# Weight sums of the seven products spread over one batch, a sliced visit one slot later, and loads and transposes in another order

## The chip, the cores and the metric

The kernel runs on one core of a Trainium2 chip. The metric is the device time of one execution in microseconds (us). Five engines take part, each with its own instruction queue: TensorE (PE, with its weight loads shown as PEld), VectorE (DVE), ScalarE (ACT), GpSimd (POOL) and SyncE (SP), which here only issues transfers.

## The reference

Eight batches of eight heads, 512 tokens of width 64 and 32 state rows per head. Tokens and state read each other by softmax attention in both directions; the two results are concatenated (544 rows per batch) and go through a feed-forward layer of width 2048 whose activation is Mish, all in float32.

```python
scores = scale * np.matmul(x, state.transpose(0, 1, 3, 2))
a = softmax(scores);  xread = np.matmul(a, state)
scores2 = scale * np.matmul(state, x.transpose(0, 1, 3, 2))
a2 = softmax(scores2); sread = np.matmul(a2, x)
x = concat(xread, sread) -> (8 * 544, 512)
h = x @ w_in                          # 512 -> 2048
g = h * np.tanh(softplus(h))          # Mish
return g @ w_out                      # 2048 -> 512
```

## The kernel before

**Precision.** Every float32 matrix product is made of three products of rounded parts: high by high, high by low, low by high. A tile and its two parts appear as `g`, `gh`, `gl` (activations), `wo` and `wx` (w_out, parts and sums), `swh`, `swl` (state times w_in) and `ah`, `al` (attention weights).

**First product.** xread @ w_in is never formed from xread: `sw_slice` multiplies a batch's state by a slice of w_in (tile `swp`), and a slot's first product (tile `ph`, 12 matmuls per slot, steps G0 and G1) multiplies the attention weights by that. For batches from 2 on w_in comes back from a DRAM copy (`load_w_in_again`, tile `w_in`, 1 MB each), two loads at a time through the tag `raw` with two buffers. The same two buffers also hold the next batch's `x_in`, its transposed form `x_turned` and its moved form `x_rows`, in this order of use: x_in, x_turned, x_rows, then the w_in loads w4, w5, w2, w3. A load can only be issued when the user of its buffer two places earlier is done.

**Slots and the table.** The work of a batch is written out in `TABLE` as eight lines, the slots, one for each pair of 128-wide parts of the feed-forward width. Each step name starts or continues one generator. The same name again means its next stage: `S4 S4 S4` is matmuls, then the copy to `swh` on ACT, then the subtraction to `swl` on DVE. PE, DVE, ACT and POOL keep the order of the program (class `InOrder`); transfers on SP are placed by the scheduler at compile time, behind what they depend on. Steps that matter here:

- G0 G1: first product into `ph`; M0 M1: Mish from `ph` on ACT, which frees the `ph` bank (two banks in all).
- A, B: half of the second product. In batch 1 these are plain products into `acc`; from batch 2 on, units `(batch, p, j)` are consumed one per A or B, as fast as they are ready.
- P, p: prepare such a unit: `gh` on ACT, `gl` on DVE and, for a unit with seven products, sums of its blocks on POOL (tile `sums`).
- S4, S6: slices of `sw` for the running batch; N0, N2: for the next. A visit S4 uses load w4.
- X0 to X3, XD: transposes of the next batch's x on DVE, and eight small transfers that move it (`x_rows`, line 305); ST: its state blocks; SC: its scores; EE, EX: exponentials on ACT (they need another activation table than Mish); NO: normalisation; PR: `at`, `ah`, `al`.
- TU (and `tu` for the batch before): `e2_turned`, two transposes on DVE into `u` and sixteen small transfers into `e2T` (line 402), which sr0 and sr1, the state reads, need two or three slots later.
- lx, li, w2 to w5: loads of x, of x_in with the state rows, and of w_in.

**Seven products.** Where a unit's j is under `sevens(key, p)`, its second product is made of seven 256-wide products in place of four 512-wide ones with two blocks each. This needs sums of weight blocks, which `seven_weights(j)` (steps T; five calls j = 0 to 4 in all) makes once for the whole kernel in three stages: an addition on DVE and four operations on POOL (tile `w_sums`, one buffer); two copies on ACT (`wo`, `wx`); two subtractions on DVE. The products of a unit are collected in four PSUM banks, and `sums_of` combines the banks `one` and `two` (a copy on ACT and three operations on DVE) before the last unit's result is added.

```python
    def sevens(key, p):
        return FIRST if (key, p) == (2, 0) else SEVEN
```

The trace gives line 74 for all operations on PE, DVE, ACT and POOL (the helper in `InOrder`), so they are told apart by tile names.

Of the kernel before, what the change touches and what calls it, by code (L numbers as in the profile page):

```python
# [17 lines left out]
P = 128  # L18
B, H, S, NS, D = 8, 8, 512, 32, 64
# [5 lines left out]
SLOTS = NFC // 2  # L25
# [2 lines left out]
WARM = 5  # L28
UNITS = 10
SEVEN = 5  # L30
FIRST = 3
G = 4 * P


# [18 lines left out]
def quad(q):  # L53
    return slice(q * NS, (q + 1) * NS)
# [27 lines left out]
def state_attention_mish_kernel(ctx, tc, x, state, w_in, w_out, out):  # L82

    nc = tc.nc
# [20 lines left out]
    def second_bank(name):  # L105
        return ps_acc.tile([P, 512], F32, tag="acc", name=name)
# [167 lines left out]
    def attention(b, sn, x_in=None):  # L274
# [115 lines left out]
        def e2_turned():  # L390

            both = pool.tile([P, NC, 2, NT, NS], F32, tag="e2T", name=f"e2T_{b}", bufs=1)
            for kc in range(2):
                e2T[kc] = both[:, :, kc]
            u = pool.tile([P, 4, 2, NT * NS], F32, tag="sc" if b else "u0", name=f"u_{b}", bufs=1)
            for kc in range(2):
                dve.transpose(
                    u[:, :, kc].rearrange("i q (t n) -> i t q n", t=NT),
                    e2s[kc].rearrange("n (t q p) -> n t q p", t=NT, q=4))
            for c in range(NC):  # L400
                for q in range(4):
                    nc.sync.dma_start(  # L402
                        both[quad(q), c].rearrange("p k t n -> p (k t n)"), u[quad(c), q].rearrange("i k m -> i (k m)"))

        two = range(2)
# [90 lines left out]
        def sread(kc):  # L496
# [18 lines left out]
        own = dict(  # L515
            x=x_transposed, st=lambda _: state_blocks(b, sn() if b == 1 else sn) if b else state_blocks_0(sn), sc=lambda _: scores() if b else scores_q(), tr=soft1_t, ex=soft1_x,
            no=lambda _: soft1_n(), pr=soft1_a, mm=soft2_m, ee=soft2_e, sr=sread, xd=lambda _: x_moved(), tu=lambda _: e2_turned(), fill=fill, aT=aT)

        def soft2():
            for kc in two:  # L520
                soft2_m(kc)
                whole(soft2_e(kc))

        own.update(soft1=soft1, parts=soft1_parts, soft2=soft2, turn=e2_turned)
        return own

# [348 lines left out]
    S1, S3, S2, S4 = range(3, 7)  # L875
    T3, T4, T2 = range(3)
# [23 lines left out]
    def products(j, n7):  # L900

        left, right = slice(0, 256), slice(256, 512)
        if j < n7:
            return [
                (A11, "one", left, wo[j][:, 0, :, left]), (S2, "one", right, wx[0][:, j, :, T2]),
                (S3, "two", left, wx[0][:, j, :, T3]), (S1, "two", right, wo[j][:, 0, :, right]),
                (A12, "top", left, wo[j][:, 1, :, left]), (S4, "top", right, wo[j][:, 1, :, right]),
                (A22, "end", left, wx[0][:, j, :, T4])]  # L910
        return [
            (a, bank, slice(0, 512), wo[j][:, k])
            for bank, blocks in (("top", (A11, A12)), ("end", (A21, A22))) for k, a in enumerate(blocks)]
# [7 lines left out]
    def sevens(key, p):  # L921
        return FIRST if (key, p) == (2, 0) else SEVEN

# [38 lines left out]
    def sums_of(key, p, banks):  # L962

        e = banks["sums"] = pool.tile([P, 4, 256], F32, tag="wt", name=f"sums_{key}_{p}", bufs=1)
        one, two = (banks[n].rearrange("t (h e) -> t h e", h=2) for n in ("one", "two"))
        act.copy(e[:, 0], one[:, 0])
        dve.tensor_sub(e[:, 3], e[:, 0], one[:, 1])
        dve.tensor_add(e[:, 1:3], two, e[:, 3:].to_broadcast([P, 2, 256]))
        dve.tensor_add(e[:, 3], e[:, 1], two[:, 1])

    def consume():

        unit = ready.pop(0)
        key, p, j = unit
        hi, lo = parts.pop(unit)
        if j == 0:
            spans[key, p] = {n: second_bank(f"acc_{key}_{p}_{n}") for n in ("one", "two", "top", "end")}
        banks = spans[key, p]
        n7 = sevens(key, p)
        if j == max(n7, SLOTS - 1 if (key, p) != (B - 1, 1) else 0):  # L980
            sums_of(key, p, banks)
        for i, (a, bank, to, w) in enumerate(products(j, n7)):
            for n, (g, h) in enumerate(((hi, 1), (hi, 0), (lo, 1))):
                fresh = (key, p, bank) not in begun_banks
                begun_banks.add((key, p, bank))
                last["PE"] = pe.matmul(
                    banks[bank][:, to], g[:, a], w[:, h], start=fresh,
                    stop=(n == 2 and (j == SLOTS - 1 and i % 2 == 1 or j == n7 - 1 and i < 4)), skip_group_check=True)
            if j == n7 - 1 == SLOTS - 1 and (i, n) == (3, 2):
                sums_of(key, p, banks)  # L990
            if j == SLOTS - 1 and i == (5 if n7 > j else 1):
                result(key, 2 * p, banks["top"], banks["sums"][:, ::2], ALU.add)
            if j == SLOTS - 1 and i == (6 if n7 > j else 3):
                result(key, 2 * p + 1, banks["end"], banks["sums"][:, 1::2], ALU.subtract)
    def result(key, t, acc, sums, op):

        acc = acc.rearrange("t (h e) -> t h e", h=2)
        for h in ((slice(0, 1), slice(1, 2)) if (key, t) == (B - 1, NT - 1) else (slice(0, 2),)):
            dve.tensor_tensor(sums[:, h], acc[:, h], sums[:, h], op)
            store(key, t, sums[:, h], out.rearrange("r (h e) -> r h e", h=2)[:, h], nc.scalar if h.start else nc.sync)  # L1000

    def half_slot(key, j, at):


        if pending:
            second((2, 3) if at else (0, 1), not at)
        elif ready and (ready[0][:2] != (key, 0) or ready[0][2] < j + (j == SLOTS - 1 and at)):
            consume()

    TABLE = {  # L1010
        1: """
            G0 M0 G1 M1 mm0 mm1 ee0 ee1 A h l X0 X1 ee0 ee1 X2 X3 XD w0
            G0 M0 G1 M1 h S2 S2 S2 B l tu ST w1
            G0 M0 G1 M1 h A B l
            G0 M0 G1 M1 h A SC sr0 sr1 S4 S6 SC sr0 sr1 S4 S4 S6 S6 lx B l MM0 MM1
            G0 M0 G1 M1 h A TR0 TR1 w2 B l TR0 TR1 T0
            G0 M0 G1 M1 EE0 EE1 EX0 EX1 h A w3 B l NO EE0 EE1 T0 T0 NO
            G0 M0 G1 M1 h A PR0 PR1 TU B l T1
            G0 M0 G1 M1 h PR0 PR1 A N0 N2 PR0 PR1 N0 N0 N2 N2 B l T1 T1 li""",
        2: """  # L1020
            G0 M0 G1 M1 X0 X1 T2 A X2 X3 XD T2
            G0 M0 G1 M1 B ST w4 A T2
            G0 M0 G1 M1 SC sr0 sr1 S4 SC sr0 sr1 S4 S4 w5 lx B P MM0 MM1 p P p
            P G0 M0 p G1 M1 P p TR0 TR1 A P TR0 TR1 p B
            P G0 M0 p G1 M1 P p A EE0 EE1 EX0 EX1 P EE0 EE1 w2 p B NO
            P G0 M0 p G1 M1 P p S6 A P NO S6 S6 w3 p B
            P G0 M0 p G1 M1 P p PR0 PR1 TU T3 A P p B T3
            P G0 M0 p T3 G1 M1 P p PR0 PR1 P A P N0 N2 PR0 PR1 N0 N0 N2 N2 p li B""",
        3: """
            P G0 M0 p G1 M1 P p X0 X1 A P X2 X3 XD p B  # L1030
            P G0 M0 p T4 G1 M1 P p ST A P T4 p w4 B T4""",
        "steady": """
            P G0 M0 p G1 M1 P p X0 X1 A P X2 X3 XD p B
            P G0 M0 p G1 M1 P p ST A P p w4 B
# [9 lines left out]
            P G0 M0 p G1 M1 P p A P SC sr0 sr1 S4 SC sr0 sr1 S4 S4 p w5 lx B MM0 MM1  # L1044
            P G0 M0 p G1 M1 P p TR0 TR1 A P TR0 TR1 p B
            P G0 M0 p G1 M1 rm P p EE0 EE1 EX0 EX1 A EE0 EE1 P rm w2 p B NO
            P G0 M0 p G1 M1 P p NO A TU P S6 S6 S6 w3 p B
            P G0 M0 p G1 M1 P p PR0 PR1 A P p B
            P G0 M0 p G1 M1 P p PR0 PR1 A P SR0 SR1 N0 N2 SR0 SR1 rs PR0 PR1 N0 N0 N2 N2 rt p W0 W1 B""",
        B - 1: """  # L1050
# [16 lines left out]
    for key in [*range(1, B - 1), "s", B - 1]:  # L1067
        if key == "s":
            for i, item in enumerate(items):
                j, r, k = i // 4, i // 2 % 2, i % 2  # L1070
# [92 lines left out]
    while ready or todo:  # L1163
        begin()
        end()
        consume()
# [24 lines left out]
```

## Time and profile before

| | |
|---|---|
| median of 3 runs | 650.94 us (650.73 to 653.28) |
| the profiled execution | 652.01 us, of which the span of the trace is 650.2 us |
| PE busy | 631.5 us (97%), granted clock 0.995 on average |
| DVE busy | 429.7 us (66%) |
| ACT busy | 311.2 us (48%) |
| POOL busy | 136.0 us (21%) |
| chain that ended last | PE 81%, DVE 9%, DMA 4%, SP's queue 3%, ACT 2% |

PE is busy nearly all the time, but a busy PE can run at half its clock, and its matmuls are pipelined. So the useful reading is the start-to-start time of the same group of matmuls at different places, with the waits that PE has between them.

### The profile page before, as it was taken

Reading aid. Unit: us, or ns where it says so; the run is one execution under the profiler, and the core shown is the slowest. Engines: PE = TensorE matmul, PEld = TensorE weight load, DVE = VectorE, ACT = ScalarE, POOL = GpSimd, SP = SyncE. Lnnn points to the kernel's source line nnn. Section 1 sums busy time; section 2 is a strip of 40 time slices with the busy share of each in tenths; the row PEclk is TensorE's granted clock in tenths of the full one; section 3 lists DMA queues with packets and bytes.
Section 4 is the critical chain, followed back from the end, with each engine's and each line's share of the span. In section 5 each row is a group of like instructions: output and inputs, shape, how many; then the busy total and the mean of one; then the engine's idle time right before and its main releaser. Section 6 shows DMA issues by size and latency. Waiting matters only on the chain.

```text
span 650.2 us, 12856 instructions
## 1 busy us (share of the span) xinstructions
PE 631.5 (97%) x5090; PEld 526.6 (81%) x5090; DVE 429.7 (66%) x737; ACT 311.2 (48%) x638; POOL 136.0 (21%) x215
## 2 busy tenths in 40 slices
PE   8999999999989989999999999999999899999997
PEld 5776787687768678888888798888888798888996
DVE  6998975568447696768476666748485776634263
ACT  5998763254235443725255433735272575424240
POOL 0000000022410434313222141405031131413130
PEclk9999999999979999999999999999999999999999
DMA  8999914701681256324562257125631240101000
GB/s 323 410 358 306 322 35 132 218 1 37 161 298 28 65 148 202 121 71 125 140 225 66 69 160 236 34 85 153 189 135 47 73 140 23 34 1 28 6 33 32
DMA packets 70123, 85.64 MB, mean 132 GB/s; under 512 B 13744, under 2 KB 48560, under 8 KB 70064
## 3 DMA queue, kind: packets, MB, share of 16 engines
q1 hardware_dynamic: 69632, 84.63, 40.5%
q8 instruction: 40, 0.66, 0.4%
q10 hardware_dynamic: 432, 0.20, 0.1%
q14 instruction: 19, 0.16, 0.1%
HBM read 59.70 MB, written 13.11 MB: 112 GB/s over the span
## 4 chain that ended last, share of the span: by engine, by line
PE 81%; DVE 9%; DMA 4%; SPq 3%; ACT 2%; issue 1%; POOL 0%; DVEq 0%; ACTq 0%
PE ph L74 23%; PE acc_top L74 12%; PE acc L74 11%; PE acc_end L74 9%; PE acc_two L74 6%; PE acc_one L74 6%; PE swp L74 4%; PE ph_s L74 3%; SPq L402 3%; DVE gl L74 2%; DMA wir<-in_moe_w_in_dram 2%; DVE swl L74 2%; DVE sums L74 1%; PE acc_s_top L74 1%; PE srp L74 1%; PE sc L74 1%
## 5 line engine op out<-in xcount | busy, mean ns | idle before, releaser
L74 ACT ACTIVATE u<-ph 128x256 f32<-128x256 f32 x192 | 63.1, 383 | 119.1 <-PE ph L74 112.3
L74 POOL TENSOR_TENSOR sums<-u 128x256 f32<-128x256 f32 x58 | 45.8, 789 | 267.8 <-DVE gl L74 266.7
L74 PE MATMUL acc_top<-wo,gh 128*128 128x256 f32 (+1 forms) x384 | 92.5, 329 | 0.0
L74 PE MATMUL ph<-ah,swh 128*128 128x512 f32 (+1 forms) x260 | 80.4, 391 | 1.8 <-DVE swl L74 1.0
L74 PE MATMUL acc<-wo,gh 128*128 128x512 f32 x256 | 81.3, 399 | 0.0
L74 PE MATMUL ph<-al,swh 128*128 128x512 f32 (+1 forms) x260 | 79.6, 388 | 0.2 <-DVE al L74 0.2
L74 PE MATMUL ph<-ah,swl 128*128 128x512 f32 (+1 forms) x260 | 79.6, 388 | 0.0
L74 PEld LDWEIGHTS acc_top<-wo,gh 128*128 128x128 f32 x384 | 63.3, 191 | 8.3 <-issue 2.1
L74 DVE TENSOR_TENSOR gl<-u,gh 128x384 fp32r<-128x384 f32 (+1 forms) x96 | 60.3, 629 | 13.3 <-ACT gh L74 9.1
L74 POOL TENSOR_TENSOR sums<-sums,u 128x128 f32<-128x128 f32 x116 | 63.5, 547 | 9.1
L74 DVE CAST gh<-u 128x512 fp32r<-128x512 f32 x38 | 17.9, 470 | 71.5 <-ACT u L74 47.5
L74 PE MATMUL acc_top<-wo,gl 128*128 128x256 f32 (+1 forms) x192 | 62.6, 326 | 0.1
L74 PEld LDWEIGHTS acc<-wo,gh 128*128 128x128 f32 x256 | 48.1, 191 | 13.6 <-issue 3.3
L74 PEld LDWEIGHTS ph<-al,swh 128*128 128x128 f32 x260 | 48.5, 188 | 10.7 <-DVE al L74 0.4
L74 PEld LDWEIGHTS ph<-ah,swh 128*128 128x128 f32 x260 | 46.7, 188 | 12.8 <-ACT g L74 1.7
L74 PEld LDWEIGHTS ph<-ah,swl 128*128 128x128 f32 x260 | 48.6, 188 | 10.4
L74 POOL TENSOR_TENSOR w_sums<-w_sums 128x256 f32<-128x256 f32 x20 | 16.6, 830 | 189.5 <-DVE w_sums L74 188.3
L74 DVE TENSOR_TENSOR swl<-swp,swh 128x512 fp32r<-128x512 f32 (+1 forms) x72 | 41.3, 623 | 22.4 <-ACT swh L74 22.4
L74 DVE TENSOR_TENSOR gl<-sums,gh 128x512 fp32r<-128x512 f32 x58 | 43.1, 743 | 17.5 <-ACT gh L74 17.5
L74 ACT CAST swh<-swp 128x512 fp32r<-128x512 f32 (+1 forms) x72 | 34.7, 549 | 35.3 <-PE swp L74 35.2
L74 PE MATMUL acc<-wo,gl 128*128 128x512 f32 x128 | 50.4, 394 | 0.0
L74 ACT CAST gh<-u 128x384 fp32r<-128x384 f32 x58 | 29.4, 515 | 43.5 <-PE acc_end L74 22.8
(173 smaller groups left out, 1256.8 us busy)
## 6 DMA issues: line engine op xcount, KB each, us to landing
w_in<-w_in_again SPq DMA_DIRECT2D x24, 1024.0 KB, 6.7
x<-in_x_dram SPq DMA_DIRECT2D x32, 256.0 KB, 6.9
wir<-in_moe_w_in_dram SPq DMA_DIRECT2D x16, 512.0 KB, 10.0
wor<-in_moe_w_out_dram SPq DMA_DIRECT2D x16, 512.0 KB, 9.6
x_rows<-x_turned SPq DMA_DIRECT2D x56, 128.0 KB, 2.4
x_in<-in_x_dram SPq DMA_DIRECT2D x24, 256.0 KB, 3.2
out_dram<-sums SPq DMA_DIRECT2D x23, 256.0 KB, 2.6
w_in_again<-w_in_sb SPq DMA_DIRECT2D x4, 1024.0 KB, 7.6
```

What stands on the lines that cost most here:

```text
L74: made = method(*args, **kwargs)
L402: nc.sync.dma_start(both[quad(q), c].rearrange("p k t n -> p (k t n)"), u[quad(c), q].rearrange("i k m -> i (k m)"))
```

## The change

1. `FIRST` goes from 3 to 5: the first span of batch 2 takes seven products for five units in place of three.
2. The five weight sums T0 to T4 move. T0 runs in slots 3 and 4 of batch 1 (was 4 and 5), T1 in slots 4 and 5 (was 6 and 7), T2 in slots 5 and 6 (was slot 7 of batch 1 and slot 0 of batch 2), T3 in slot 7 and slot 0 of batch 2 (was slots 6 and 7 of batch 2), T4 in slots 1 and 2 of batch 2 (was slot 7 of batch 2 and slot 1 of batch 3). Line 3 of the table becomes the common one.
3. S4 of batch 2 goes from slot 2 to slot 3, after A.
4. `tu` of batch 1 is called one slot earlier (slot 0), and four of its sixteen transfers are issued from ACT's queue.
5. `sums_of` comes one unit earlier (j = 6 in place of 7) for all spans but the first of batches 2 and 6; the last span keeps its place.
6. In batch 6, slot 5, the visit S6 and the load w3 come ahead of TU.

```diff
-FIRST = 3
+FIRST = 5
...
             for c in range(NC):
                 for q in range(4):
-                    nc.sync.dma_start(
+                    (nc.sync if b != 1 or q else nc.scalar).dma_start(
                         both[quad(q), c].rearrange("p k t n -> p (k t n)"), u[quad(c), q].rearrange("i k m -> i (k m)"))
...
-        if j == max(n7, SLOTS - 1 if (key, p) != (B - 1, 1) else 0):
+        if j == max(n7, SLOTS - 1 if (key, p) in ((2, 0), (B - 2, 0)) else 0 if (key, p) == (B - 1, 1) else SLOTS - 2):
             sums_of(key, p, banks)
...
     TABLE = {
         1: """
-            G0 M0 G1 M1 mm0 mm1 ee0 ee1 A h l X0 X1 ee0 ee1 X2 X3 XD w0
-            G0 M0 G1 M1 h S2 S2 S2 B l tu ST w1
+            G0 M0 G1 M1 mm0 mm1 ee0 ee1 A h l X0 X1 ee0 ee1 X2 X3 XD tu w0
+            G0 M0 G1 M1 h S2 S2 S2 B l ST w1
             G0 M0 G1 M1 h A B l
-            G0 M0 G1 M1 h A SC sr0 sr1 S4 S6 SC sr0 sr1 S4 S4 S6 S6 lx B l MM0 MM1
-            G0 M0 G1 M1 h A TR0 TR1 w2 B l TR0 TR1 T0
-            G0 M0 G1 M1 EE0 EE1 EX0 EX1 h A w3 B l NO EE0 EE1 T0 T0 NO
-            G0 M0 G1 M1 h A PR0 PR1 TU B l T1
-            G0 M0 G1 M1 h PR0 PR1 A N0 N2 PR0 PR1 N0 N0 N2 N2 B l T1 T1 li""",
+            G0 M0 G1 M1 h A SC sr0 sr1 S4 S6 SC sr0 sr1 S4 S4 S6 S6 lx B l MM0 MM1 T0
+            G0 M0 G1 M1 h T0 A TR0 TR1 w2 B l T0 TR0 TR1 T1
+            G0 M0 G1 M1 T1 EE0 EE1 EX0 EX1 h A w3 B l T1 NO EE0 EE1 T2 NO
+            G0 M0 G1 M1 h T2 A PR0 PR1 TU B l T2
+            G0 M0 G1 M1 h PR0 PR1 A N0 N2 PR0 PR1 N0 N0 N2 N2 B l T3 li""",
         2: """
-            G0 M0 G1 M1 X0 X1 T2 A X2 X3 XD T2
-            G0 M0 G1 M1 B ST w4 A T2
-            G0 M0 G1 M1 SC sr0 sr1 S4 SC sr0 sr1 S4 S4 w5 lx B P MM0 MM1 p P p
-            P G0 M0 p G1 M1 P p TR0 TR1 A P TR0 TR1 p B
+            G0 M0 G1 M1 X0 X1 A X2 X3 XD T3 T3
+            G0 M0 G1 M1 T4 B ST w4 T4 A
+            G0 M0 G1 M1 T4 SC sr0 sr1 SC sr0 sr1 w5 lx B P MM0 MM1 p P p
+            P G0 M0 p G1 M1 P p A S4 TR0 TR1 S4 S4 P TR0 TR1 p B
             P G0 M0 p G1 M1 P p A EE0 EE1 EX0 EX1 P EE0 EE1 w2 p B NO
             P G0 M0 p G1 M1 P p S6 A P NO S6 S6 w3 p B
-            P G0 M0 p G1 M1 P p PR0 PR1 TU T3 A P p B T3
-            P G0 M0 p T3 G1 M1 P p PR0 PR1 P A P N0 N2 PR0 PR1 N0 N0 N2 N2 p li B""",
-        3: """
-            P G0 M0 p G1 M1 P p X0 X1 A P X2 X3 XD p B
-            P G0 M0 p T4 G1 M1 P p ST A P T4 p w4 B T4""",
+            P G0 M0 p G1 M1 P p PR0 PR1 TU A P p B
+            P G0 M0 p G1 M1 P p PR0 PR1 P A P N0 N2 PR0 PR1 N0 N0 N2 N2 p li B""",
...
         B - 2: """
...
-            P G0 M0 p G1 M1 P p NO A TU P S6 S6 S6 w3 p B
+            P G0 M0 p G1 M1 P p NO A P S6 w3 TU S6 S6 p B
```

## Rows read from the trace of the kernel before

**Rows 1.** Waits of PE over the whole span: us in total, times, longest.
```profile
PE swp L74 <- DMA w_in<-w_in_again: 5.3, 2, 4.4
PE srp L74 <- DMA e2T<-u: 1.3, 1, 1.3
...
PE acc_two L74 <- DVE sums L74: 0.7, 4, 0.2
PE acc_one L74 <- DVE sums L74: 0.6, 1, 0.6
```
**Rows 2.** Timeline of PE, batch 2, slot 2 to slot 3: start, us.
```profile
175.41 1.09 PE L74 MATMUL sc<-x_rows,bd 64*32 64x256 f32 x32
...
181.90 1.96 PE L74 MATMUL swp<-w_in,bd 64*32 64x256 f32 x32 [4.36 <-DMA w_in<-w_in_again]
...
188.22 0.63 PE L74 MATMUL ph<-ah,swh 128*128 128x512 f32 x2
```
**Rows 3.** Chain that ended last, batch 6, in order of time: start, us.
```profile
450.28 2.75 PE ph L74 x12
...
458.06 2.75 PE ph L74 x12
...
463.32 1.02 PE sc L74 x32
...
469.35 2.72 PE ph L74 x12
...
477.51 2.72 PE ph L74 x12
```
**Rows 4.** Two stretches of PE: us, busy (instructions), granted clock, DMA share, GB/s.
```profile
116.80:118.40 1.60, 0.34 (x14) 1.00 0.16 41
...
181.90:183.90 2.00, 2.00 (x33) 0.50 1.06 403
```
**Rows 5.** Timeline of SP's issues, end of batch 1 to batch 2.
```profile
150.14 10.86 SPq L402 DMA_DIRECT2D e2T<-u  x16
161.10 2.07 SPq L136 DMA_DIRECT2D x_in<-in_x_dram  x4
167.79 5.21 SPq L305 DMA_DIRECT2D x_rows<-x_turned  x8
...
174.93 0.59 SPq L568 DMA_DIRECT2D w_in<-w_in_again  x1
```
**Rows 6.** Timeline of PE, slot 7 to slot 0: batches 2 to 3, and 3 to 4.
```profile
221.67 1.09 PE L74 MATMUL swp<-w_in,bd 64*32 64x256 f32 x32
...
229.53 0.73 PE L74 MATMUL ph<-ah,swh 128*128 128x512 f32 x2 [0.97 <-DVE swl L74]
...
296.26 1.96 PE L74 MATMUL swp<-w_in,bd 64*32 64x256 f32 x64
...
301.04 0.62 PE L74 MATMUL ph<-ah,swh 128*128 128x512 f32 x2
```
**Rows 7.** Timeline of ACT: batch 1, slot 5 (three rows), and batch 2, slot 7.
```profile
137.20 0.73 ACT L74 ACTIVATE e<-scs,nm 128x512 f32<-128x512 f32 x1
...
138.63 1.13 ACT L74 ACTIVATE e<-e 128x512 f32<-128x512 f32 x2
...
141.90 1.28 ACT L74 ACT_TABLE_LOAD   x1
...
222.19 0.83 ACT L74 CAST wx<-w_sums 128x768 fp32r<-128x768 f32 x1 [2.10 <-POOL w_sums L74]
```
**Rows 8.** Timeline of DVE, batch 1, slots 4 to 6.
```profile
136.13 1.22 DVE L74 TENSOR_TENSOR w_sums<-wo 128x1024 f32<-128x1024 f32 x1
...
142.01 0.67 DVE L74 TENSOR_REDUCE s<-e 128x16 f32<-128x512 f32 x1
...
148.85 1.26 DVE L74 STREAM_TRANSPOSE u<-e 128x512 f32<-128x512 f32 x2
```
**Rows 9.** Timeline of POOL, the first weight sums.
```profile
137.50 3.51 POOL L74 TENSOR_TENSOR w_sums<-w_sums 128x256 f32<-128x256 f32 x4 [136.19 <-DVE w_sums L74]
```

## Prediction

> **What bounds the kernel.** I read the page first: PE is busy 97% of the span and holds 81% of the chain that ended last, so only two things can shorten the time, fewer PE cycles or fewer and shorter PE stalls. The second view is therefore the list of PE's waits [rows 1]. It sums to little, some 15 µs at the start and everywhere else, but one entry stands out: 4.4 µs for a load of w_in. The third view is the timeline of PE there [rows 2]: in batch 2 the scores start at 175.41, S4 waits from about 177.5 to 181.90, and the next slot's first product starts at 188.22. The same stretch in a quiet batch, with S4's kind of visit in it, is 469.35 - 463.32 = 6.03 µs in the chain [rows 3]; here it is 12.81. So that wait costs 6.8 µs, not 4.4. The rest, 2.3 µs beside small restarts, is the clock [rows 4]: after the 4.36 µs wait PE ran at a granted 0.50 (1.2 GHz), while in the 1.3 µs wait at 117 it stayed at 1.00 (2.4 GHz). The Trainium skill's page "TensorE: Matmul & The Clock Gate", section "What's actually happening", ties the two levels to how busy PE has lately been; these rows agree.
>
> The cause of the load's lateness is read from SP's queue [rows 5]. Sixteen issues for e2T take 10.86 µs (0.68 each) from 150.14; x_in is next, though its buffer was free earlier; the transposes, eight moves (5.21 µs) and at 174.93 load w4 follow; S4 begins 7.0 µs later. What starts e2T's issues is the end of `u` on DVE. The fourth view is slot 7 of batch 2 [rows 6]: from the first visit to the next slot's first product takes 229.53 - 221.67 = 7.86 µs, in the next batch 301.04 - 296.26 = 4.78. The 3.1 µs more are T3's: ACT's copy to `wx` waited for POOL until 222.19 [rows 7], and Mish, which frees the banks, and `swh`, `swl` are behind it in ACT's and DVE's order.
>
> **The change, part by part.**
>
> *S4 one slot later.* The 6.8 µs go if w4 has landed by then. Its new place is behind the state reads, B, G and A: from the start of SC about 2.1 + 3 x 2.72 = 10.3 µs. w4 follows the first x_rows issue by 174.93 - 167.79 = 7.1 µs and needs 7.0 to land; SC itself needs those moves landed (at the latest where w4 was issued, 7.1 after the first). So w4 lands 7.0 after SC can start, 3.3 µs before S4: however late this chain is, S4 doesn't wait. **-6.8.**
>
> *T3 and T4 out of batches 2 and 3.* The 3.1 µs of [rows 6] go; the places that T3 gets (slot 7 of batch 1, its copies in slot 0, the subtractions behind X3) have no visit behind them. **-3.1.** T4's copies wait for POOL in slot 1 and may hold Mish of slot 2; that is hidden by SC's wait, below.
>
> *T0.* Its addition follows slot 3's last work on DVE, which was idle then until Mish of the next slot; its copies stand in slot 4, where ACT only has two Mish steps. I cost them at nothing; without that cover, 0.83 µs for a copy.
>
> *T1 ahead of the exponentials.* Here is the cost. In slot 4 T0's subtractions come before the turned scores' maxima. They have 1024 columns like the addition, so an estimate of 1.2 µs. T1's addition then ends at 136.13 + 1.22 + 1.22 = 138.6 [rows 8], POOL's four operations (3.51) [rows 9] at 142.1, the copy on ACT (0.83) at 142.9, the table load (1.28) at 144.2. Only then the exponentials start, 7.0 µs later than at 137.20 [rows 7]. They had ended at 139.8 while NO began at 142.01, so part is absorbed: the first EX now ends at 146.2, NO begins 4.2 later. Between NO's stages T2's addition (1.22) takes the place of T0's subtractions. So `u` and e2T's first issue come 4.2 µs later, near 154.4, and x_in with them. T2 is no longer between the transposes of x (1.1 back), so x_rows is 3.1 later and SC can start at 167.79 + 3.1 + 7.1 = 178.0 against 175.41. **+2.6.** Bounds: 0, if the scheduler puts x_in ahead of e2T; about 4, if the operations on DVE before `u` are slowed or one more stage of T falls ahead of it. I take the worked value, since SP kept this order in the trace.
>
> *T2.* Its copies stand ahead of Mish of slot 7 in ACT's queue, and the visit N2 needs both `ph` banks. That is T3's pattern over again, 0.5 to 0.9 µs of wait for PE. It costs nothing on its own: SC, two and a half slots later, starts when x_rows lands, and PE now waits there for some 2 µs. If x_rows were early, it would show.
>
> *tu earlier, four transfers on ACT.* The 1.3 µs wait of the state reads [rows 1], 1.4 with its restart: four issues fewer on SP are 4 x 0.68 = 2.7 µs. The Trainium skill's page "DMA: Bandwidth & Descriptors", section "Rules for kernel authors", says that spreading transfers over SP and ACT gives no bandwidth and saves only issue time. Here the issue time is what is late [rows 5], so that rule leaves the sum as it is. **-1.4**, bounds 0 and -1.4. ACT has gaps of several µs between Mish steps in slots 1 and 2; were the issues put ahead of a Mish step, up to 2.7.
>
> *Five sevens.* Two units in seven products: (458.06 - 450.28 - 2.75) / 2 = 2.52 µs a unit against (477.51 - 469.35 - 2.72) / 2 = 2.72 [rows 3]. **-0.4.** Each also puts sums on POOL and one more copy on ACT, and S4's `swl` now has only B between it and the next G. Between nothing and the 0.97 µs that PE waited for `swl` in [rows 6]; I take **+0.6**, as POOL must serve units 2 to 4 in a row.
>
> *sums_of earlier.* PE waits for it 0.7 in four places and 0.6 in one [rows 1]. Three of the four are first spans of batches 3 to 5, now one unit earlier: 0.5; the 0.6 stands right behind T3's late DVE work, and goes with it. **-1.1**, bounds 0 and -1.3.
>
> *Batch 6.* w3 ahead of TU should end the second wait for w_in (5.3 - 4.4 = 0.9 µs). I take nothing: in the same slot PE then has to wait for the splitting of the state reads on ACT and DVE, which starts from the state reads and not from w3. Bounds 0 and -0.9.
>
> Sum: -6.8 - 3.1 + 2.6 - 1.4 - 0.4 + 0.6 - 1.1 = **-9.6 µs**. The profiled execution's 652.01 would become 642.4. It lies 1.07 above the median of the runs, so against the median I predict 650.94 - 9.6 = **641.3 µs**.
>
> **The rivals.**
>
> *x_in is not late* (order on SP, or exponentials not held by T1's copies). For: SP places transfers at compile time. Against: in the trace e2T goes first. Then the +2.6 is not paid: 638.7.
>
> *The wait at SC drops the clock.* It is some 2 µs by my count, between the 1.3 that left the clock at 1.00 and the 4.36 that ended at 0.50 [rows 4]. Nearer to the first, so not forecast; its price is the 2.3 µs of [rows 2]: 643.6.
>
> *sums_of gets in the way.* In slot 7 its copy and three operations now stand ahead of `al` and `swl`, which the next slot's first product needs. Ten spans have it earlier; if each made PE wait 0.7 µs, 7 µs go back: 648.3, no change that can be told. Against: `swl` in [rows 6] had time in the quiet batch, no wait stands at 301.04.
>
> *Slower.* The lateness of e2T's issues goes to SC one for one. If T1 and T2 each held DVE's chain for a whole slot (8.2 µs, [rows 3]), `u` would be 16.3 late and not 4.2: 12.1 more, and with the clock's 2.3 the sum is +4.8: 655.7. It decides from about 14 µs of lateness on. Against: only the POOL operations, 3.5 µs each, stand in the way.
>
> **How the numbers follow.** Forecast 0.52, x_in not late 0.18, clock 0.17, sums_of 0.08, slower 0.05. The measurement can tell about 0.5%, 3.3 µs. The first three are faster by more: 0.87; the fourth is within: 0.08; slower: 0.05. The range takes in the first three with their bounds: low 638.7 less most of batch 6's 0.9, 638.0; high 643.6 with 1.4 more lateness, 0.4 more in batch 2 and 1.1 not gained, 646.5.
>
> **What would show it.** S4 without a wait and no stretch at 0.50 after it; a wait of about 2 µs at SC of batch 2 for x_rows; e2T's issues of batch 1, slot 6 starting some 4 µs later against the first products; exponentials behind a copy to `wx`; slot 7 of batch 2 at 4.8 µs; the state reads at 117 without a wait. The prediction is wrong if SC waits 4 µs or more, if S4 still waits, or if PE shows new waits in slots 3 to 6 of batch 2 or for `swl` at the starts of batches.

## The result and the profile after

The changed kernel takes **644.27 us** (median of 4 runs, 643.92 to 646.52), against 652.11 us of the kernel before in the same session (4 runs, 650.73 to 653.94): a ratio of 0.9885, 95% interval 0.9848 to 0.9923, about 7.5 us less by the ratio. The forecast was 641.3 us with a range of 638.0 to 646.5. Its profiled execution took 644.3 us with a span of 642.5 us, where before's had 650.2.

The list of PE's waits, to be read beside [rows 1] (total in us, times, longest):

```profile
PE srTp L74 <- DVE swl L74: 2.1, 1, 2.1
PE ph L74 <- ACT g L74: 1.4, 2, 1.1
...
PE sc L74 <- issue: 1.2, 2, 0.7
PE ph L74 <- DVE swl L74: 1.2, 1, 1.2
...
PEld sc L74 <- DMA x_rows<-x_turned: 1.2, 1, 1.2
```

Both entries of [rows 1] that carried the argument, w_in with 5.3 and e2T with 1.3, are gone, and acc_two's 0.7 in four places is 0.2 in one. The four entries of PE shown here are small, none above 2.1; the one on srTp, in batch 6, was 0.8 before. The other three stand, but for 0.4 us at the start of the kernel, in one stretch, the end of batch 1 and the start of batch 2. PE's timeline there, from slot 7 of batch 1 to slot 3 of batch 2, answers to [rows 2]:

```profile
148.91 0.74 PE L74 MATMUL ph<-ah,swh 128*128 128x512 f32 x2 [1.05 <-ACT g L74]
...
155.85 1.58 PE L74 MATMUL swp<-w_in,bd 64*32 64x256 f32 x32 [0.19 <-ACT g L74]
...
161.55 0.72 PE L74 MATMUL ph<-ah,swh 128*128 128x512 f32 x2 [1.18 <-DVE swl L74]
...
178.70 0.59 PE L74 MATMUL sc<-x_rows,bd 64*32 64x256 f32 x2 [0.51 <-issue]
...
180.00 1.09 PE L74 MATMUL sc<-x_rows,bd 64*32 64x256 f32 x30 [0.72 <-issue]
181.03 1.10 PE L74 MATMUL srp<-x,e2T 128*32 128x64 f32 x64
...
190.24 1.09 PE L74 MATMUL swp<-w_in,bd 64*32 64x256 f32 x32
```

S4, the visit at 190.24, has no wait, and the stretch around it ran at full clock, where [rows 4] showed 0.50 (columns as there, with the busy times of all engines):

```profile
190.00:192.00 2.00, 2.00 (x41) 1.33 (x40) 1.23 (x2) 1.75 (x5) 0.99 (x2) 1.00 1.10 387
```

The scores at 178.70 and 180.00 are late for x_rows: PE's own line names no releaser, but their weight loads (PEld, above) wait 1.2 us for its moves. SP's issues show why these are late, beside [rows 5]:

```profile
155.61 10.58 SPq L402 DMA_DIRECT2D e2T<-u  x16
166.29 2.07 SPq L136 DMA_DIRECT2D x_in<-in_x_dram  x4
172.87 5.20 SPq L305 DMA_DIRECT2D x_rows<-x_turned  x8
```

Executions differ by up to 3 us in the loads ahead of batch 1, so kernels are compared here from one PE instruction to another. In us:

| stretch | before | after | difference | forecast |
|---|---|---|---|---|
| scores of batch 1 to state reads of batch 2 | 60.64 | 64.62 | +4.0 | +1.2 |
| state reads of batch 2 to the first product of slot 4 | 19.56 | 12.85 | -6.7 | -6.8 |
| slots 4 and 5 of batch 2 | 14.69 | 14.25 | -0.4 | -0.4 |
| slot 6 | 5.44 | 5.91 | +0.5 | +0.6 |
| slot 7, to the first product of batch 3 | 13.40 | 10.31 | -3.1 | -3.1 |
| slot 0 of batch 3 | 9.22 | 8.18 | -1.0 | -0.6 |
| slots 0 of batches 4 to 6, together | 24.5 | 23.3 | -1.2 | -0.5 |

From the state reads of batch 2 to the end of the span the difference is 473.76 - 461.47 = 12.3 us of gain (forecast 10.8), of which the rows of the table hold 11.9; ahead of them 4.0 are lost (forecast 1.2).

### The profile page after: what moved, and what is told of

It is laid out like the page before. It is cut to its first block, busy times and chain, and to the rows that moved or that the text cites. A ratio compares the mean times of both kernels' runs of the same rounds, so it can differ in the third digit from the quotient of the medians.

```text
span 642.5 us, 12893 instructions
## 1 busy us (share of the span) xinstructions
PE 628.8 (98%) x5108; PEld 526.5 (82%) x5108; DVE 431.2 (67%) x737; ACT 313.7 (49%) x642; POOL 141.5 (22%) x221
## 4 chain that ended last, share of the span: by engine, by line
PE 86%; DVE 6%; ACT 3%; DMA 3%; POOL 1%; issue 1%; SPq 0%; DVEq 0%; ACTq 0%; POOLq 0%
PE ph L74 24%; PE acc_top L74 14%; PE acc_end L74 11%; PE acc L74 9%; PE acc_two L74 6%; PE acc_one L74 6%; PE swp L74 4%; PE ph_s L74 3%; DMA wir<-in_moe_w_in_dram 2%; PE sc L74 2%; PE srp L74 1%; PE acc_s_top L74 1%; DVE swl L74 1%; PE acc_s_end L74 1%; DVE gl L74 1%; ACT L74 1%
## 5 line engine op out<-in xcount | busy, mean ns | idle before, releaser
L74 POOL TENSOR_TENSOR sums<-u 128x256 f32<-128x256 f32 x60 | 48.1, 802 | 283.6 <-DVE gl L74 276.1
L74 POOL TENSOR_TENSOR sums<-sums,u 128x128 f32<-128x128 f32 x120 | 66.1, 551 | 9.4
L74 DVE TENSOR_TENSOR gl<-sums,gh 128x512 fp32r<-128x512 f32 x60 | 46.7, 779 | 18.6 <-ACT gh L74 18.6
L74 PEld LDWEIGHTS ph<-al,swh 128*128 128x128 f32 x260 | 48.5, 188 | 10.8 <-DVE al L74 0.4
L74 ACT CAST gh<-u 128x384 fp32r<-128x384 f32 x60 | 30.7, 514 | 39.6 <-issue 19.2
```

What stands on the lines that cost most here:

```text
L74: made = method(*args, **kwargs)
```

## The experiments

Each kernel is the changed one with one edit, unless said otherwise. Times are medians, beside 651.7 to 651.9 us of the kernel before on the same chips.

**S4's place.** The kernel before with S4 alone moved:

```diff
-SC sr0 sr1 S4 SC sr0 sr1 S4 S4 w5 ... | ... P p TR0 TR1 A P
+SC sr0 sr1 SC sr0 sr1 w5 ...          | ... P p A S4 TR0 TR1 S4 S4 P
```

> The kernel before with one edit: S4 of batch 2 goes from slot 2 to slot 3, behind A. Theory (the wait and the half clock behind it both go, 12.81 us becomes 6.03): 6.7 us faster, ratio about 0.990, no wait of PE for w_in in batch 2. Rival (the wait only moves, since w5 and the next loads queue behind w4, or only the 4.4 us of waiting come back): 0 to 4.4 us faster.

Measured 646.50 us, ratio 0.9918 (0.9902 to 0.9934): 5.3 us faster. From the state reads of batch 2 to the end it took 468.25 us against 473.76. That is 1.2 short of 6.7, and a later stage lost more than this: from the state reads of batch 6, slot 7, to the first product on them it took 9.61 us, against 8.01 before, at half clock behind waits of 0.8 and 1.0. The row of that stretch (columns as above):

```profile
508.00:510.00 2.00, 2.00 (x6) 1.55 (x5) 2.00 (x5) 1.61 (x4) 0.18 (x1) 0.50 0.00 0
```

The reverse, the changed kernel with S4 back in slot 2:

> The changed kernel with S4 of batch 2 back in slot 2. Theory: w4, issued near 180 and 7 us on its way, ends a wait of about 4.9 us, PE comes out of it at half clock, in all about 7 us slower than the changed kernel and about level with the kernel before. Rival (with SC already late for x_rows, w4 is no longer what is missing): under 3 us slower.

Measured 652.44 us, ratio 0.9997 (0.9978 to 1.0016, 10 runs): no gain is left. S4 waits again, in PE's timeline of this kernel:

```profile
188.70 1.96 PE L74 MATMUL swp<-w_in,bd 64*32 64x256 f32 x32 [5.04 <-DMA w_in<-w_in_again]
```

And the clock is halved behind the wait, in its windows, columns as in [rows 4]:

```profile
188.70:190.70 2.00, 2.00 (x33) 0.50 1.06 394
```

So this step decides the sign: with S4 in its old place the rest of the change gains nothing that can be measured.

**T1's place.** T1's copies and subtractions behind the exponentials and the normalisation:

```diff
-G0 M0 G1 M1 T1 EE0 EE1 EX0 EX1 h A w3 B l T1 NO EE0 EE1 T2 NO
+G0 M0 G1 M1 EE0 EE1 EX0 EX1 T1 h A w3 B l NO T1 EE0 EE1 T2 NO
```

> The changed kernel with T1's copies on ACT behind the exponentials of slot 5 and its subtractions on DVE behind NO's first stage. Theory (T1's copies, waiting for POOL, hold the exponentials, and from them NO, u, e2T's issues, x_in, x_rows and SC follow): e2T's issues start some 6 us earlier, the 1.05 us wait at the start of slot 7, the 1.2 us for swl at the start of batch 2 and the 2 us around SC go, 4 to 5.5 us faster than the changed kernel, near 639.5. Rival (SC is late by the queue of SP and the landing of x_in, or by DVE and POOL slowing one another wherever T1 stands): under 1.5 us faster.

Measured **639.70 us** (638.94 to 640.61), ratio 0.9814 (0.9799 to 0.9829): 4.6 us faster than the change, the best kernel of the study. The first stretch is 59.75 us against 64.62. PE's three waits are gone there, though the scores' matmuls still take 1.8 us in place of 1.1, and e2T and x_in are issued close to their times in [rows 5]:

```profile
150.52 10.96 SPq L402 DMA_DIRECT2D e2T<-u  x16
161.58 2.08 SPq L136 DMA_DIRECT2D x_in<-in_x_dram  x4
167.58 5.19 SPq L305 DMA_DIRECT2D x_rows<-x_turned  x8
```

Half of it alone, the copies behind the exponentials and the subtractions still ahead of NO:

```diff
-G0 M0 G1 M1 T1 EE0 EE1 EX0 EX1 h A w3 B l T1 NO
+G0 M0 G1 M1 EE0 EE1 EX0 EX1 T1 h A w3 B l T1 NO
```

> The changed kernel with T1's copies on ACT behind the exponentials, but its subtractions on DVE still ahead of NO, where they wait for the copy to wx. Theory (both queues carry the wait on): NO starts near 144 against the first products of slot 6, 2.5 us earlier than in the changed kernel and 3 later than in t1_behind, so about half of the 4.6 us. Rival (ACT's order alone): the same time as t1_behind.

The stretch is 61.85 us, so 2.8 of the 4.9 come from ACT's order and 2.1 from DVE's: NO now waits behind the subtraction from `wx`. The time, 644.12 us (0.9869, 0.9837 to 0.9902), doesn't show it. In the profiled execution (645.19 us) two stretches at a granted 0.50 lie outside the experiment, one at 60 to 65 us and one in batch 6; of the four executions the only one with a mean granted clock of 1.000 took 641.54 us, against 644.30 for the changed kernel's.

T1's and T2's four operations each on DVE in place of POOL:

```diff
+        by = dve if j in (1, 2) else pool_e
-        pool_e.tensor_sub(w[:, 0], w[:, 0], w[:, 1])
+        by.tensor_sub(w[:, 0], w[:, 0], w[:, 1])
...
```

> The changed kernel with the four operations of T1 and of T2 on DVE in place of POOL, their places in the program kept. If POOL's 4.5 us for T1 (3.5 forecast) and the doubled operations on DVE beside it make the lateness: exponentials 2 to 3 us earlier, u about 2 us earlier, SC 2 us earlier, 2 to 3 us faster than the changed kernel. If the order alone counts and POOL's speed does not: no change, or slower by the 3.3 us that DVE then has more.

The stretch is 62.15 us (-2.5), the time 643.25 us (0.987, 0.9855 to 0.9886). The same four operations take 1.81 us on DVE, against 4.50 (T1) and 3.83 (T2) on POOL, and the operations of DVE that ran beside T2 on POOL are short again. The changed kernel's timeline of DVE, while POOL works (150.61 to 154.44):

```profile
150.66 1.23 DVE L74 TENSOR_TENSOR e<-e,r 128x512 f32<-128x512 f32 x1
151.81 1.22 DVE L74 CAST gh<-g 128x1024 fp32r<-128x1024 f32 x1
```

The same operations in the timeline of the kernel with T1 and T2 on DVE:

```profile
148.78 1.80 DVE L74 TENSOR_TENSOR w_sums<-w_sums 128x256 f32<-128x256 f32 x4
150.78 0.69 DVE L74 TENSOR_TENSOR e<-e,r 128x512 f32<-128x512 f32 x1
151.39 0.69 DVE L74 CAST gh<-g 128x1024 fp32r<-128x1024 f32 x1
```

x_in for batch 3 issued from ACT, so that it doesn't queue behind e2T on SP:

```diff
-last["load"] = nc.sync.dma_start(xs[:, c], x[b] ...
+last["load"] = (by or nc.sync).dma_start(xs[:, c], x[b] ...   # by = nc.scalar for b == 3
```

> The changed kernel with the four loads of x_in for batch 3 issued from ACT, not behind e2T's sixteen issues on SP. Theory (SC is late because x_in waits in SP's queue behind e2T): x_in is issued some 6 us earlier, x_rows right behind e2T, the waits around SC and the 2 us they cost go; the waits at slot 7 (1.05) and for swl (1.2) stay: about 2 us faster than the changed kernel. Rival (SC waits for something else, the chain from T1 through DVE and the aT parts alone): no change around SC.

643.28 us (0.9868, 0.9838 to 0.9902); the stretch is 62.71 us (-1.9). The scores run in one piece, as x_rows is 5.5 us earlier while e2T is not:

```profile
155.55 11.70 SPq L402 DMA_DIRECT2D e2T<-u  x16
167.36 5.18 SPq L305 DMA_DIRECT2D x_rows<-x_turned  x8
```

The waits of 1.05 and 1.18 in slots 7 and 0 stay. Where the time of the first stretch goes is read from the lengths of its slots, from one first product to the next, in us (slots 4 and 5 of batch 1 and slot 1 of batch 2 take 8.16 in all four kernels):

| | before | after | x_in on ACT | T1 behind |
|---|---|---|---|---|
| batch 1, slot 6 | 8.16 | 9.38 | 9.38 | 8.16 |
| batch 1, slot 7 | 10.31 | 12.64 | 12.64 | 10.31 |
| batch 2, slot 0 | 5.44 | 5.59 | 5.58 | 5.44 |
| batch 2, slot 2, to the state reads | 3.84 | 5.73 | 3.83 | 4.56 |

So T1's place costs 3.7 us in slots 6 to 0, by way of ACT and DVE, and 1.9 at the scores, by way of SP's queue, 5.6 in all. x_in on ACT takes back the 1.9; T1 behind the exponentials takes back the 3.7 and 1.2 of the 1.9, together the 4.9.

**T3 and T4** back in batches 2 and 3 (diff cut to these steps; `|` stands between lines of the table):

```diff
-FIRST = 5
+FIRST = 3
-... N2 N2 B l T3 li                                                       # batch 1, slot 7
+... N2 N2 B l li
-X2 X3 XD T3 T3 | T4 B ST w4 T4 A | T4 SC                                   # batch 2, slots 0 to 2
+X2 X3 XD       | B ST w4 A       | SC
+PR0 PR1 TU T3 A P p B T3 | P G0 M0 p T3 G1 M1 P p | p T4 G1 M1 ... T4 p w4 B T4   # slots 6, 7; batch 3
```

> The changed kernel with T3 and T4 back in slots 6 and 7 of batch 2 and in batch 3, and FIRST back at 3, as both need. Theory (T3's copies wait for POOL ahead of Mish in slot 7): slot 7 of batch 2 takes 3.1 us longer again, the start of batch 3 0.9, the two units 0.4, less up to 0.5 that slot 6 gains: 4 us slower than the changed kernel. Rival (the 3.1 us came from the late chain of the old slot 2 and not from T3): under 1 us slower.

648.91 us, ratio 0.9950 (0.993 to 0.9971): 4.6 us slower than the change. From the state reads of batch 2 to the end it takes 466.50 us against 461.47; slot 7 of batch 2 and slot 0 of batch 3 have 4.1 of these 5.0 (13.41 and 9.21 us, as before), and slot 7 shows the pattern of [rows 6], in PE's timeline:

```profile
219.52 1.09 PE L74 MATMUL swp<-w_in,bd 64*32 64x256 f32 x32
221.50 1.64 PE L74 MATMUL swp<-w_in,bd 64*32 64x256 f32 x32 [0.89 <-ACT u L74]
...
227.40 0.73 PE L74 MATMUL ph<-ah,swh 128*128 128x512 f32 x2 [0.94 <-DVE swl L74]
```

**FIRST = 3 alone.**

```diff
-FIRST = 5
+FIRST = 3
```

Units 3 and 4 of batch 2's first span then read blocks of w_out that T3 and T4 have by then replaced by sums, so that part is another product; the work and its order are as before.

> The changed kernel with FIRST at 3. Theory: units 3 and 4 take 2.72 us and not 2.52, and slot 6 loses its wait of about 0.45 us for swl, since POOL and ACT have less to do: 0 to 0.4 us slower. Rival (the sums for two more units hold PE): 0.5 us faster or more.

643.92 us (0.9879, 0.9856 to 0.9903): no change. Slots 4 and 5 are 0.45 us longer (8.01 and 6.69 against 7.78 and 6.47), slot 6 is 0.47 shorter, without its wait for `swl`. Five sevens buy nothing; what FIRST = 5 does is to let T3 and T4 overwrite those blocks earlier.

**sums_of** one unit later again in all spans but the last:

```diff
-SLOTS - 1 if (key, p) in ((2, 0), (B - 2, 0)) else 0 if (key, p) == (B - 1, 1) else SLOTS - 2
+SLOTS - 1 if (key, p) != (B - 1, 1) else 0
```

> The changed kernel with sums_of at j = 7 again for every span but the last. Theory: three starts of batches take 0.55 us longer each, the rest little: 1.7 to 2.1 us slower. Forecast's term: 0.5 us slower. Rival (sums_of one unit earlier gets in the way of swl in slot 7): 0 to 7 us faster.

645.84 us (0.9902, 0.9877 to 0.9927): the intervals overlap, but the trace is plain. Batch 4's slot 0 takes 8.17 us against 7.75, PE waits for `acc_two` 0.6 us in four places together, and from the state reads of batch 2 to the end it is 1.3 us longer.

**e2T of batch 1** all on SP, tu still in slot 0:

```diff
-(nc.sync if b != 1 or q else nc.scalar).dma_start(
+nc.sync.dma_start(
```

> The changed kernel with all sixteen transfers of e2T in batch 1 on SP again; tu stays in slot 0. Theory (SP's issues are what is late, and x_rows' moves go ahead of them, so the earlier call alone buys nothing): the last issue is 2.5 us later, the state reads wait 0.7 to 1.1 us, about 1 us slower. Rival (the earlier slot does it): no wait, no change.

644.57 us (0.9899, 0.9869 to 0.9929): no change in the time. The state reads wait 0.32 us, not 1.33 as before, and from the scores to the sliced visit behind them it takes 2.64 us, against 3.64 before and 2.06 after. The earlier call alone puts e2T ahead of two stores on SP, which stood in front of it. SP's timeline before:

```profile
105.88 1.03 SPq L679 DMA_DIRECT2D out_dram<-o  x2
107.01 10.07 SPq L402 DMA_DIRECT2D e2T<-u  x16
```

And in this kernel:

```profile
105.78 10.05 SPq L402 DMA_DIRECT2D e2T<-u  x16
115.93 1.00 SPq L679 DMA_DIRECT2D out_dram<-o  x2
```

**Batch 6.** Slot 5's old order:

```diff
-NO A P S6 w3 TU S6 S6 p B
+NO A TU P S6 S6 S6 w3 p B
```

> The changed kernel with batch 6 slot 5 in the old order (TU ahead of w3). Theory of the prediction (its new order is worth nothing, as PE then waits for the splitting of the state reads): the wait for w_in of 0.9 us comes back and the wait on srTp falls from 2.07 to 0.8, the stretch from the state reads to the first product on them stays at 8.0, time 643.6 to 645.0. Rival (what matters is the clock, which falls behind one wait of 2.07 us in some executions but not behind two of 0.9 and 0.8): time up to 1 us less than the changed kernel, 643.0 to 643.8. Third (the w_in wait is a loss of its own): 0.9 more, 645.2.

644.82 us (642.59 to 647.23; ratio 0.9888, 0.9865 to 0.9911). The wait for w_in is back with 0.57 and the one on srTp falls to 1.18; state reads to first product take 8.01 us, as in the kernel before (8.01) and after (8.03). This edit is worth nothing, as forecast; the second theory, about the clock, got no support from the time.

The best kernel with the wait on srTp attacked, N0's splitting and the transpose ahead of A's splitting:

```diff
-SR0 SR1 rs PR0 PR1 N0 N0 N2 N2 rt p W0 W1 B
+SR0 SR1 rs N0 N0 rt PR0 PR1 N2 N2 p W0 W1 B
```

> The kernel with T1 behind the exponentials, and in batch 6, slot 7, the state reads' transpose directly behind N0's splitting, with A's splitting for the next batch (al, 1.3 us on DVE) and N2's behind it. In that kernel PE waited 2.07 us for swl before the transpose, and in its profiled execution the granted clock fell to 0.50 behind the wait for 3.3 us; in the profile of the changed kernel the same 2.07 us left it at 1.00. Theory (the loss behind batch 6 is this wait, and in some executions the clock behind it): the wait shrinks to about 0.9, the clock stays at 1.00, the stretch from the state reads of slot 7 to the first product on them is 6.8 to 7.0 us against 8.03 with the clock at 1.00 and 9.65 at 0.50; time 637.0 to 638.6, against 639.7. Rival (ph_s waits for the splitting of the state reads or of w_in anyway): the stretch stays at 8.0, time 639.0 to 640.0.

640.34 us (639.7 to 642.55; ratio 0.9828, 0.9806 to 0.9849): not faster than 639.70. Nor is it at full clock: its executions with a mean granted clock of 1.000 took 639.7 to 640.34 us, the one of the kernel with T1 behind 638.94. The theory was right on the wait (0.90) and on the stretch (6.80 us), the rival nearer on the time: the next thing is late, `wl`, behind the same work on DVE. PE's timeline in this kernel:

```profile
500.40 0.33 PE L74 MATMUL srTp<-ident,srds 128*128 128x128 f32 x1 [0.90 <-DVE swl L74]
...
503.32 1.14 PE L74 MATMUL ph_s<-srT,wh 128*128 128x512 f32 x4
...
505.48 0.74 PE L74 MATMUL ph_s<-srT,wl 128*128 128x256 f32 x4 [1.02 <-DVE wl L74]
506.06 1.09 PE L74 MATMUL ph_s<-srT,wh 128*128 128x512 f32 x4
```

From the state reads to the second group of ph_s it is 506.06 - 496.52 = 9.54 us, in the changed kernel 509.79 - 500.37 = 9.42.

## Why the prediction came out as it did

**S4: right, -6.7 of -6.8.** The step named both halves, the wait and the 2.3 us of half clock behind it, and undoing the step alone brings both back.

**T3 and T4: right, -3.1**, and slot 0 of batch 3 is 1.0 us shorter too: its wait of 0.6 for `acc_one` is gone, the one for `acc_two` stays at 0.16. With the step undone both slots are back at their lengths of before, so the step is worth 4.1 us.

**T0: right, nothing.** Slots 4 and 5 of batch 1 take 8.16 us before and after.

**T1 ahead of the exponentials: right in mechanism, mis-sized.** This is the step that failed. The term was +2.6 with a bound of about 4; with the state reads' gain of 1.6 us taken out of the +4.0 it measured +5.6. The prediction took POOL's four operations and the operations of DVE at the lengths that they had in the trace of before; where the new order put them beside each other, both took longer.

To compare the times of the two traces, they are taken against the same first product: slot 4 of batch 1 starts at 124.21 before and at 123.21 in the changed kernel, so a forecast time stands 1.0 us earlier there. T1's addition ends at 137.56, which is the forecast's 138.6. Then POOL took 4.50 us for T1, not 3.51 as in [rows 9], and ACT's copy waited for it. The exponentials start at 144.38; the forecast's 144.2 stands for 143.2 here, so they are 1.2 us late. POOL's and ACT's timelines of the changed kernel:

```profile
137.70 4.50 POOL L74 TENSOR_TENSOR w_sums<-w_sums 128x256 f32<-128x256 f32 x4 [7.20 <-DVE w_sums L74]
...
142.24 0.83 ACT L74 CAST wx<-w_sums 128x768 fp32r<-128x768 f32 x1 [3.04 <-POOL w_sums L74]
143.09 1.28 ACT L74 ACT_TABLE_LOAD   x1
144.38 0.72 ACT L74 ACTIVATE e<-scs,nm 128x512 f32<-128x512 f32 x1
```

Behind them two more things went otherwise. From the start of NO to `u` the forecast had 6.84 us, as in [rows 8]; it took 154.32 - 146.46 = 7.86, since T2's operations now ran on POOL beside NO and two operations of DVE took 1.2 us in place of 0.69. Slowed operations of DVE were the prediction's way to its bound of about 4; that POOL is slowed too was not in it. The trace of before had a sign of this that the prediction did not read: of its five groups on POOL, the one of [rows 9] took 3.51 us beside a DVE that mostly waited, and the next one 4.15:

```profile
152.50 4.15 POOL L74 TENSOR_TENSOR w_sums<-w_sums 128x256 f32<-128x256 f32 x4 [11.50 <-DVE w_sums L74]
...
166.69 3.18 POOL L74 TENSOR_TENSOR w_sums<-w_sums 128x256 f32<-128x256 f32 x4 [10.05 <-DVE w_sums L74]
```

So e2T's first issue, behind `u`, was 6.5 us later against the first products, and not 4.2 (32.40 us behind the start of slot 4, before 25.93). And of the 1.1 us that T2 was to give back between the transposes of x only 0.4 came: from e2T's first issue to x_rows' it takes 172.87 - 155.61 = 17.26 us, before 17.65. With T2 gone the transposes wait for x_in to land, as DVE's timeline of the changed kernel has it:

```profile
171.47 1.37 DVE L74 STREAM_TRANSPOSE x_turned<-x_in 128x512 f32<-128x512 f32 x2 [0.82 <-DMA x_in<-in_x_dram]
```

So x_rows was 6.1 us later and not 3.1. The last step was right: x_rows' first issue plus 7.1 is 179.97, and the scores' second part starts at 180.00. The prediction's own list of signs had one for this step, a new wait for `swl` at the start of a batch; batch 2 has it, 1.18 us.

**T2's copies: right in kind, too small.** Foretold were 0.5 to 0.9 us of wait; slots 7 and 0 have 1.05 (Mish of slot 6 behind the late exponentials and their table load), 0.19 and 1.18 (T2's copy, which waited 2.69 us for POOL), and slots 6 to 0 are 3.7 us longer. T2's own place is not the cause: with T1 behind the exponentials T2 stands where it stood, and none of these waits is left. That they cost nothing on their own here, since the scores are late for x_rows anyway, is the prediction's argument, and no run takes them away alone. With the scores in time they do cost: 62.71 us with x_in on ACT against 59.75 with T1 behind.

**tu and ACT's issues: right size, wrong cause.** From the scores of batch 1 to the sliced visit behind the state reads it is 118.47 - 116.41 = 2.06 us against 119.44 - 115.80 = 3.64: -1.6, forecast -1.4. But 1.0 of it comes from the earlier call and only 0.6 from the four issues on ACT, as the run with all sixteen on SP shows with its 2.64. By the rule of the Trainium skill's page "DMA: Bandwidth & Descriptors", section "Rules for kernel authors", spreading saves only issue time; these 0.6 us agree with it.

**Five sevens -0.4, new in batch 2 +0.6: right**, -0.4 and +0.5; the two cancel.

**sums_of: the gain was undervalued.** The term of -1.1 held 0.5 for the starts of batches 4 to 6 and 0.6 for `acc_one`, which went with T3 as said. The three starts gained 1.2 us, not 0.5, and with sums_of late again the stretch behind the state reads is 1.3 longer. Each wait of 0.16 cost 0.41 of its slot; what the other 0.25 are, no run shows.

**Batch 6: right, nothing.** The wait for w_in (0.94) is gone and the one on srTp went from 0.81 to 2.07; the stretch is 8.03 us, before 8.01.

**The rivals.** x_in was late. The clock did not fall at the scores. sums_of got in nobody's way. The slower case was far off: e2T was 6.5 us late, not 14.

**The sum.** Ahead of the state reads 2.8 us more were lost than forecast. Behind them 1.5 us more were gained than forecast, 0.4 in slot 0 of batch 3, 0.7 by sums_of and the rest in no one place. That these offset half of the miss is luck; without them the time would be some 645.8 us, still inside the range but close to its end.

## What to carry to other kernels

Price a stall from start to start between two instructions that both kernels have, not by its length: 4.4 us of wait were 6.8 us here, 0.2 were 0.4. Work that is "free" on another engine is free only until something that PE needs stands behind it in that engine's order; the same weight sums cost 5.6 us ahead of the exponentials and 0.7 behind them. A count that takes an engine's operations at the length they had in another place is too low where the new order puts two engines side by side: T1's four took 4.50 us and not 3.51. When a producer is late, follow the issue queue: e2T's sixteen issues made x_in late, x_in the transposes, and these the scores, each with its own delay, and slack between two of them counts only if the later one doesn't wait for a landing.

## What the runs showed of the hardware

**POOL and DVE slow each other.** Four 128x256 operations on POOL took 4.50 us beside DVE's casts and subtractions, and 3.18 to 4.15 us in the five groups of before, of which [rows 9] is one; a 128x512 multiplication on DVE went from 0.69 to 1.23 us beside them and a 128x1024 cast from 0.69 to 1.22. The run with the sums on DVE puts both back to 0.69. That DVE's work lengthens POOL's is read from these groups alone; no run takes DVE's work away from beside POOL. The Trainium skill's page "GPSIMD Engine Reference", section "1. Specifications", says that the two share their SBUF interfaces, with contention where a DVE instruction has two SBUF inputs or runs in a 2-port mode. The multiplication, with two inputs, agrees with it; the cast has one, and no row shows its mode. Either was about 0.5 us longer.

**The same wait does not always cost the clock.** PE waited 2.07 us for srTp in batch 6, in the changed kernel and in the one with T1 behind. In the changed kernel the granted clock stayed at 1.00 behind it. Its timeline of PE has the wait:

```profile
505.49 0.33 PE L74 MATMUL srTp<-ident,srds 128*128 128x128 f32 x1 [2.07 <-DVE swl L74]
```

And its windows, columns as in [rows 4], the clock:

```profile
505.49:507.00 1.51, 1.51 (x7) 1.00 0.00 0
507.00:509.00 2.00, 2.00 (x10) 1.00 0.04 8
```

With T1 behind, the timeline shows the same wait:

```profile
500.15 0.33 PE L74 MATMUL srTp<-ident,srds 128*128 128x128 f32 x1 [2.07 <-DVE swl L74]
```

But its windows fall to 0.50, from about 501 to 504.5 us:

```profile
501.00:502.00 1.00, 1.00 (x4) 0.61 0.00 0
502.00:503.00 1.00, 1.00 (x4) 0.50 0.00 0
```

From the state reads to the first product on them this makes 9.65 us in place of 8.03. Four of the profiled executions show some 9.6 there (S4 alone behind two waits, T1 behind, its half, T1 on DVE), the nine others that keep the order of this slot 8.0 to 8.5. It is most of the spread that remained behind the state reads of batch 2 between kernels alike there: without these 1.6 us the three with T1 changed take 461.4 to 461.5 us from the state reads of batch 2 to the end, as the changed kernel does (461.47). The Trainium skill's page "TensorE: Matmul & The Clock Gate", section "What's actually happening", calls what the gate watches free-running, and its effect at the start of a kernel run-variable; that one wait of 2.07 us in mid-kernel has both outcomes agrees with it. Waits of 4.36 and 5.04 us ended at 0.50; which wait of 1 to 2 us will is not settled by these runs.
